# A two-stage mixture-of-experts kernel: part of the second to last expert's slots written back as whole rows by one scatter

## The chip, the cores and the metric

The kernel runs on one core of one Trainium2 chip. The metric is the device time of one execution in microseconds (us). Engines are named as the profile names them: PE is TensorE's matmul, PEld its weight load, DVE VectorE, ACT ScalarE, POOL GpSimd, SP SyncE. A small q behind a name (POOLq) is the engine's sequencer.

## What is computed

Three stages follow each other: attention in which a query sees the keys of its own hash bucket, a mixture of eight experts with one expert per token, and one with two experts per token. The change lies in the last stage, whose reference is, cut to its core:

```python
N, D, E, F = 1536, 512, 8, 1024
for e in range(E):
    for k in range(2):
        mask = top2[:, k] == e
        h = np.maximum(x[mask] @ w1[e], 0.0)
        out[mask] += top2_w[mask, k, None] * (h @ w2[e])
```

So each row of `out` (512 numbers for one token) is the sum of two experts' weighted rows.

## The kernel before

**Slots.** The tokens of an expert of the second mixture are collected in DRAM (`xs2`) in a list of `CAP2` = 416 slots per expert, of which `USE2` = 408 are computed. A slot is a row of 512 numbers, the token's number and its eight expert weights. Empty slots hold a token number out of range, which an indirect DMA drops.

**One expert of the second mixture (key 8 + e).** `x2_load` (L1315 on) and `x2_rest` (L1323) load the slots' rows and the small columns behind them. Everything is computed with the model dimension on the partitions: `mm1` (L1142 to L1144) gives four pairs of hidden blocks of 128 x 408, each product in three matmuls of split float32 parts; ACT's ReLU (L1151) and DVE's residual (L1155) split each pair and free its PSUM buffer (two buffers "S"). `mm2` (L1177 to L1179) gives four output blocks `Y` of 128 x 408; ACT copies each to SBUF (`ys`, L1202) and fills the last 8 columns (L1204). ACT and DVE also split each expert's weights (L272, L278).

**Writing back, experts 0 to 6.** `y2_turn` (L1360) turns each of the four `ys` on DVE in blocks of 32 x 32 into `yo`, so that a partition holds a quarter of a token's row for each of NQ = 13 groups of 32 slots. `y2_weight` (L1365) multiplies by the expert weight, in three parts (5, 4 and 4 groups). `y2_add` (L1368) issues one indirect DMA on POOL for each group: 128 quarter rows of 512 bytes, added to `out` by the DMA. The experts' weight columns are laid out on the host so that the quarters come out in order.

**Writing back, expert 7 (the last).** It adds on the core instead. `y2_gather` (L1342) gathers four lots of 104 rows of `out` into SBUF by indirect DMAs on POOL; they need all of expert 6's scatters to have landed. `y2_tr` (L1351) turns three lots of output on PE into PSUM; the fourth is computed by `mm2_rows` (L1189 to L1191) with tokens on the partitions, in two halves. `y2_sum` (L1356) and `y2_half` (L1196) on DVE form weight x output + gathered row, and `y2_put` (L1379) writes whole rows by four plain indirect DMAs on POOL. These puts are the last work of the kernel.

**The order.** Instructions are not issued in the order of the source. A planner (`Plan`, L104) takes steps with an engine, an expected length, a due time, dependences and buffers, and simulates the engines: each engine takes of the steps that could start within a small time (`WAITS2`, per engine) the one with the earliest due time. `LENGTH` and `LENGTH2` replace expected lengths, `SHIFT` and `SHIFT2` shift due times of groups of steps. One plan orders attention and routing (`LENGTH`, `SHIFT`, `WAITS`), a second all sixteen experts (`LENGTH2`, `SHIFT2`, `WAITS2`). What comes out is the order of each engine's queue, in which the chip then works strictly.

Of the kernel before, what the change touches and what calls it, by code (L numbers as in the profile page):

```python
# [9 lines left out]
F32 = mybir.dt.float32  # L10
F32R = mybir.dt.float32r
I32 = mybir.dt.int32
U32 = mybir.dt.uint32
AF = mybir.ActivationFunctionType
OP = mybir.AluOpType
# [6 lines left out]
N, D, E, F = NB * S, NHEAD * DH, 8, 1024  # L22
# [3 lines left out]
CAP2 = 416  # L26
USE2 = 408
MB = CAP2 // 4
ML = USE2 - 3 * MB
NQ = CAP2 // 32  # L30
RW1 = D + 2 + E
RW2 = D + 1 + E
# [5 lines left out]
HOP = {("PE", "ACT"): 260, ("PE", "DVE"): 280, ("ACT", "DVE"): 149, ("ACT", "POOL"): 195, ("DVE", "POOL"): 169,  # L38
       ("POOL", "ACT"): 86, ("ACT", "PE"): 165, ("DVE", "PE"): 228, ("DVE", "SP"): 110, ("POOL", "DVE"): 80,
       ("DVE", "ACT"): 150, ("POOL", "PE"): 100, ("ACT", "SP"): 60, ("POOL", "SP"): 60, ("PE", "POOL"): 280}  # L40
LENGTH = {('X4', 'at', 5600): 6800, ('ACT', 'ph0', 412): 407, ('DVE', 'pl0', 469): 466, ('DVE', 'pl', 469): 477, ('DVE', 'sp', 433): 806, ('ACT', 'fk0', 733): 727,
# [31 lines left out]
SHIFT2 = {'g1a': -95, 'g1b6': -110, 'g1b7': -110, 'g2a': -175, 'g2b6': -80, 'g3a': -235, 'g3b6': -25, 'g4a': 5, 'g4b6': -140,  # L73
# [3 lines left out]
    'rhd': -135, 'rla': -10, 'rlb': -25, 'rlc': 98, 'rld': 75, 'sqa': -35, 'sqb6': -15, 'wh0a': -28, 'wh0b': 7.3,  # L77
    'wh0c': 10, 'wh1a': -20.5, 'wh1b': -100, 'wh1c': -20, 'wl0a': -31.3, 'wl0b': -5, 'wl0c': -65, 'wl1a': -14, 'wl1b': 45.4,
    'wl1c': 85, 'wr0a': -40, 'wr0b': -45, 'wr1a': -90, 'wr1b': -150, 'wr1c': 250, 'xha': -20, 'xhb': -12.003557058503825, 'xhc': 97,
    'xla': -55, 'xlb': -200, 'xloa': -10, 'xloc': 85, 'xmb': -155, 'xmc': 70, 'xta': -75, 'xtb': 41, 'yc0a': -280,  # L80
    'yc0b': -100, 'yca': -27, 'ycb': 35, 'ycc': 73, 'ycd': 50, 'yra': -25, 'yrb6': -2, 'yrb7': -65, 'ywd': 94}
WAITS2 = {'PE': (0, 0), 'ACT': (325, 0), 'DVE': (120, 0.47396423297385304), 'POOL': (1495, 0)}
WAIT = 120
ROUTING = ("rsa", "rsb", "r7", "rm", "rr0", "rr", "rq", "rp", "rn", "rv", "re", "rg", "ra", "rc", "ro", "xa", "xb", "oh", "xo")
PR = dict(sc=-5.4, mx=-8.7, ex=-5.34, pv=3.37, fin=3.38, bits=-14.64, prep=-18.57, load=-37.69, h=-17.66, l=0)
# [18 lines left out]
class Plan:  # L104
# [8 lines left out]
    def add(self, name, eng, dur, fn, due, deps=(), use=(), new=(), lat=0):  # L113
        t = self.length.get((eng, name[0], dur), dur)
        dur, lat = t if isinstance(t, tuple) else (t, lat)
        due += self.shift.get(self.group(name, eng), 0)
        self.steps[name] = (eng, dur, fn, due, tuple(deps), tuple(use) + tuple(new), tuple(new), lat)
# [68 lines left out]
def lsh_attention_moe_moe2_kernel(  # L186
# [4 lines left out]
    nc = tc.nc  # L191
    xd = tc.dram_tile([N, D], F32, name="xd")
    xs1 = tc.dram_tile([E * N, RW1], F32, name="xs1")
    xs2 = tc.dram_tile([E * N, RW2], F32, name="xs2")
# [3 lines left out]
    psp = main.enter_context(tc.tile_pool(name="psp", bufs=1, space=PSUM))  # L198
# [18 lines left out]
    idf = con.tile([128, 128], F32, name="idf")  # L217
# [227 lines left out]
    ap = lambda n, b: att.enter_context(tc.tile_pool(name=n, bufs=b))  # L445
    ld, wk, hl = ap("ld", 2), ap("wk", 2), ap("hl", HLN)
    acon, rt, rows = ap("acon", 1), ap("rt", 2), ap("rows", 1)
# [411 lines left out]
    add = plan.add  # L859
    P = lambda f, *a, **k: (lambda: f(*a, **k))  # L860
    for i, t in enumerate((3150, 3700, 3900, 4500, 5600, 6200, 6300)):
        add(("at", i), f"X{i}", t, lambda: None, -100,
            new=[(r, i // 4) for r in ("qk", "vr")] if i in (0, 4) else [])
    FIRST0 = [[("fk0",), ("fv", 0), ("hc0",), ("fv1", 0), ("fa", 0, 0)], [("hc", 0), ("fv1", 1), ("fa", 0, 1)]]
    FIRST = [[], [("mx", 0, 0)], [("mx", 0, 1)], [("mx", 0, 2)]]
    for h in range(HEADS):
        z = 12 * h
        due = lambda k, o=0.0: z + PR[k] + o
        if h > 1:
            add(("load", h), "SP", 1800, P(loads, h), due("load"), [("load", h - 1)] if h > 2 else [], lat=4500,  # L870
                new=[("qk", h), ("vr", h)])
        ld_ = ([("load", h)] if h > 1 else [("at", 4)]) + ([("ph", h - 1)] if h else [])
        nq = []
        if h == 0:
            lo, hi = slice(0, 64), slice(64, 128)
            R = [("qk", 0), ("hx", 0), ("qa", 0)]
            for c in range(2):
                add(("ph0", c) if c == 0 else ("ph", 0), "ACT", 412, P(first_h, c), -40 + c, [("at", c)], use=R if c else [],
                    new=[] if c else [("hx", 0), ("qb", 0), ("qa", 0)] + nq)
# [19 lines left out]
        else:  # L899
            add(("ph", h), "ACT", 733, P(prep_h, h), due("prep"), ld_, use=[("qk", h)], new=[("hx", h)] + nq)  # L900
            add(("hc", h), "SP", 2500, P(prep_hcopy, h), due("prep", .1), [("ph", h)], lat=3500,
                use=[("hx", h)], new=[("qb", h), ("qa", h)])
            for c in range(4):
                add(("pl", h, c), "POOL", 552, P(prep_l, h, c), due("prep", .2 + .1 * c),
                    [("ph", h)] + ([("pl", h, c - 1)] if c else []),
                    use=[("qk", h), ("hx", h)] + ([("lx", h)] if c else []), new=[] if c else [("lx", h)])
            add(("lc", h), "SP", 1250, P(prep_lcopy, h), due("prep", 1), [("pl", h, 3), ("hc", h)], lat=3000,
                use=[("lx", h), ("qb", h)])
# [414 lines left out]
    def x2_rest(e):  # L1323
        x = XM[8 + e] = yp.tile([128, NQ, RW2 - D], F32, name="xm2", bufs=3)
        if e < E - 1:
            for a in range(4):
                nc.sync.dma_start(x[32 * a:32 * a + 32], xs2[e * N:e * N + CAP2].rearrange("(b j) c -> j b c", j=32)[:, :, D:])
        else:
            nc.sync.dma_start(x[:MB, :4], xs2[e * N:e * N + CAP2].rearrange("(b p) c -> p b c", p=MB)[:, :, D:])

    def x2_meta(e):
        if e < E - 1:
            IDX[e] = yp.tile([128, NQ], I32, name="idx", bufs=3)
            nc.vector.tensor_scalar(IDX[e], XM[8 + e][:, :, 0], 4.0, quarter, op0=OP.mult, op1=OP.add)
            return
        IDX[e] = yp.tile([128, NQ], I32, name="idx", bufs=3)[:, :4]
        nc.vector.tensor_copy(IDX[e][:MB], XM[8 + e][:MB, :4, 0])
        WC[e] = yp.tile([128, 4], F32, name="wc")
        nc.vector.tensor_copy(WC[e][:MB], XM[8 + e][:MB, :4, 1 + e])
# [16 lines left out]
        nc.vector.scalar_tensor_tensor(o[:MB], P[:MB], w, GA[0][:MB, b * D:b * D + D], op0=OP.mult, op1=OP.add)  # L1356

    def y2_turn(e, d):

        nc.vector.transpose(YT[e][:, :NQ * 128].rearrange("p (b c) -> p b c", c=128)[:, :, d * 32:d * 32 + 32],  # L1360
                            YS[8 + e, d].rearrange("p (b j) -> p b j", j=32))

    def y2_weight(e, bs):
        y = YT[e][:, :NQ * 128].rearrange("p (b c) -> p b c", c=128)[:, bs]
# [55 lines left out]
    add(("gm",), "POOL", 1742, ga_new, Z[15] - 5, [("xl", 15)], new=[("xr", "ga")])  # L1420
    add(("go",), "X", 7500, lambda: None, -98)
    add(("yob",), "X1", 0, P(yt_new, "b"), -98, new=[("yo", "b")])
    add(("yo7",), "X2", 0, P(yt_new, E - 1), Z[15], [("ps", E - 2, b) for b in range(NQ)], new=[("yo", E - 1)])
    add(("iw",), "POOL", 1100, iw_init, -20)
    add(("go0",), "X0", GO, lambda: None, -98)
    for n in range(4, 128):
# [13 lines left out]
    for key in range(2 * E):  # L1440
# [120 lines left out]
        else:  # L1561
            for d in range(4 if e < E - 1 else 0):
                add(("yt", key, d), "DVE", 502, P(lambda e, d: ([yt_new(e)] if d == 0 else 0, y2_turn(e, d)), e, d), z + q * (11 + 2 * d), [("yc", key, d)] + [("yt", key, 0)] * (d > 0),
                    use=[("ys", (key, d))] + [("yo", e)] * (d > 0), new=[("yo", e)] if d == 0 else [])
            for c in range(3 if e < E - 1 else 0):
                bs = slice((0, 5, 9)[c], (5, 9, 13)[c])
                add(("yw", key, c), "DVE", 60 + 134 * (bs.stop - bs.start), P(y2_weight, e, bs), t + c, [("yt", key, d) for d in range(4)] + [("xm", key)],
                    use=[("yo", e), ("xm", e)])
                for b in range(bs.start, bs.stop):
                    add(("ps", e, b), "POOL", 1850, P(y2_add, e, b), t + b, [("yw", key, c)],  # L1570
                        use=[("yo", e), ("ix", e)], lat=2000)
            for b in range(4 if e == E - 1 else 0):
                add(("ga", e, b), "POOL", 1038, P(y2_gather, e, b), z + 8 + (b + 1) % 4,
                    [("xm", key), ("gm",)] + [("ps", e - 1, c) for c in range(NQ)], use=[("ix", e), ("xr", "ga")], lat=2000)
                O = ("O" if b % 2 else "ET", ("o", e, b))
                if (e, b) == (E - 1, 3):
                    for p in range(2):
                        O = ("ET", ("last", p))
                        add(("yt", key, b, p), "PE", 2560, P(mm2_rows, p), t + p,
                            [("rl", key, c) for c in range(4)] + [("m2", key, 3, 1)] + [("yt", key, b, 0)] * p,  # L1580
                            use=[("w1", key * 8 + 4 + 2 * p + c) for c in range(2)] + [("hh", (key, c)) for c in range(4)], new=[O])
                        add(("yo", e, b) if p else ("yo0",), "DVE", 330, P(y2_half, p), t + p, [("yt", key, b, p), ("ga", e, b), ("yo7",)] + [("yo0",)] * p,
                            use=[O, ("ix", e), ("yo", e), ("xr", "ga")])
                else:
                    add(("yt", key, b), "PE", 434, P(y2_tr, e, b), t + (1.5 * b if e < E - 1 else .2), [("yc", key, d) for d in range(4)],
                        use=[("ys", (key, d)) for d in range(4)], new=[O])
                    add(("yo", e, b), "DVE", 663, P(y2_sum, e, b), t + 1.5 * b, [("yt", key, b), ("ga", e, b), ("yo7",)],
                        use=[O, ("ix", e), ("yo", e), ("xr", "ga")])
                add(("ps", e, b), "POOL", 1038, P(y2_put, e, b), t + 1.5 * b, [("yo", e, b)],
                    use=[("yo", e), ("ix", e)], lat=2000)  # L1590
# [142 lines left out]
```

## Time and profile before

| | us |
|---|---|
| median of three runs | 756.21 |
| lowest and highest | 755.67, 757.37 |
| the profiled execution | 756.93 |
| its span in the trace | 755.2 |

The span runs from the first to the last instruction that the trace shows. A row of a timeline gives start, duration, engine, line, operation with output and inputs, count, and in brackets how long the engine had been idle and what released it.

### The profile page before, as it was taken

Reading aid. Unit: us, or ns where it says so; the run is one execution under the profiler, and the core shown is the slowest. Engines: PE = TensorE matmul, PEld = TensorE weight load, DVE = VectorE, ACT = ScalarE, POOL = GpSimd, SP = SyncE. Lnnn points to the kernel's source line nnn. Section 1 sums busy time; section 2 is a strip of 40 time slices with the busy share of each in tenths; the row PEclk is TensorE's granted clock in tenths of the full one; section 3 lists DMA queues with packets and bytes.
Section 4 is the critical chain, followed back from the end, with each engine's and each line's share of the span. In section 5 each row is a group of like instructions: output and inputs, shape, how many; then the busy total and the mean of one; then the engine's idle time right before and its main releaser. Section 6 shows DMA issues by size and latency. Waiting matters only on the chain. (4 is left out here: it accounts for less than half of the span.)

```text
span 755.2 us, 14504 instructions
## 1 busy us (share of the span) xinstructions
PE 738.8 (98%) x4827; PEld 718.9 (95%) x4827; DVE 570.1 (75%) x1251; ACT 473.8 (63%) x1037; POOL 381.9 (51%) x664
## 2 busy tenths in 40 slices
PE   8999999999999999999999999999999999999995
PEld 6999999999999899999999999999999999999994
DVE  7989989999998868988978868576676656664411
ACT  7889989898878747755657745456444444444310
POOL 6543445566666550334124352046657484858474
PEclk9999999999999999999999999999999999999998
DMA  7687887888765369786687766969979595956133
GB/s 196 185 211 216 218 216 198 245 221 202 169 159 165 137 198 256 231 258 203 197 260 207 232 213 196 208 175 260 185 180 210 133 204 136 192 126 116 14 34 85
DMA packets 142117, 140.61 MB, mean 186 GB/s; under 512 B 25901, under 2 KB 122437, under 8 KB 142037
## 3 DMA queue, kind: packets, MB, share of 16 engines
q1 hardware_dynamic: 124789, 122.94, 59.5%
q0 software_dynamic: 17248, 16.69, 11.3%
q8 instruction: 40, 0.66, 0.4%
q14 instruction: 40, 0.33, 0.2%
HBM read 88.54 MB, written 34.44 MB: 163 GB/s over the span
## 5 line engine op out<-in xcount | busy, mean ns | idle before, releaser
L1368 POOL DMA_INDIRECT out_dram<-yo,idx x91 | 152.0, 1670 | 114.7 <-DVE yo L1365 89.1
L1142 PE MATMUL S<-xh,w0h 128*128 128x224 f32 (+1 forms) x512 | 161.8, 316 | 0.0
L1143 PE MATMUL S<-xl,w0h 128*128 128x224 f32 (+1 forms) x512 | 159.1, 311 | 0.0
L1144 PE MATMUL S<-xh,w0l 128*128 128x224 f32 (+1 forms) x512 | 159.0, 311 | 0.0
L1151 ACT ACTIVATE hh<-S 128x448 fp32r<-128x448 f32 (+1 forms) x64 | 44.6, 697 | 108.2 <-PE S L1144 105.6
L698 DVE TENSOR_TENSOR el<-ET,eh 128x384 fp32r<-128x384 f32 x192 | 99.2, 551 | 6.3 <-ACT eh L692 4.8
L692 ACT ACTIVATE eh<-ET 128x384 fp32r<-128x384 f32 x192 | 91.0, 496 | 16.9 <-PE ET L688 16.4
L680 ACT ACTIVATE es<-S,mxs 128x768 f32<-128x768 f32 x96 | 95.9, 999 | 8.1 <-POOL mxs L676 4.8
L670 DVE TENSOR_REDUCE mxs<-S 128x1 f32<-128x768 f32 x96 | 91.6, 954 | 12.3 <-PE S L665 9.3
L1155 DVE SCALAR_TENSOR_TENSOR hh<-S,hh 128x448 fp32r<-128x448 f32 (+1 forms) x64 | 51.9, 811 | 62.2 <-ACT hh L1151 62.1
L1143 PEld LDWEIGHTS S<-xl,w0h 128*128 128x128 f32 x512 | 97.2, 190 | 0.5 <-DVE xl L1128 0.5
L1142 PEld LDWEIGHTS S<-xh,w0h 128*128 128x128 f32 x512 | 97.4, 190 | 0.0
L1144 PEld LDWEIGHTS S<-xh,w0l 128*128 128x128 f32 x512 | 97.2, 190 | 0.0
L278 DVE TENSOR_TENSOR w1l<-wraw,w1h 128x512 fp32r<-128x512 f32 x128 | 82.7, 687 | 11.4 <-ACT w1h L272 11.2
L688 PE MATMUL ET<-idf,es 128*128 128x128 f32 x576 | 90.0, 274 | 1.0 <-DVE el L698 1.0
L1178 PE MATMUL ET<-hh,w1h 128*128 128x408 f32 (+2 forms) x264 | 89.8, 340 | 0.0
L1179 PE MATMUL ET<-hh,w1l 128*128 128x408 f32 (+2 forms) x264 | 89.7, 340 | 0.0
L1177 PE MATMUL ET<-hh,w1h 128*128 128x408 f32 (+2 forms) x264 | 89.1, 338 | 0.0
L272 ACT ACTIVATE w1h<-wraw 128x512 fp32r<-128x512 f32 x128 | 73.2, 623 | 21.9 <-PE ET L1178 9.9
L272 ACT ACTIVATE w0h<-wraw 128x512 fp32r<-128x512 f32 (+1 forms) x152 | 78.4, 560 | 3.3 <-DMA wraw<-in_w1a_dram 1.6
L278 DVE TENSOR_TENSOR w0l<-wraw,w0h 128x512 fp32r<-128x512 f32 x120 | 77.7, 686 | 3.6 <-ACT w0h L272 3.1
L688 PEld LDWEIGHTS ET<-idf,es 128*128 128x128 f32 x576 | 71.1, 142 | 8.6 <-DVE el L698 1.5
(272 smaller groups left out, 1591.4 us busy)
## 6 DMA issues: line engine op xcount, KB each, us to landing
wraw<-in_w1a_dram SPq DMA_DIRECT2D x32, 512.0 KB, 4.1
wraw<-in_w2a_dram SPq DMA_DIRECT2D x32, 512.0 KB, 6.0
wraw<-in_w1b_dram SPq DMA_DIRECT2D x32, 512.0 KB, 4.8
wraw<-in_w2b_dram SPq DMA_DIRECT2D x32, 512.0 KB, 5.9
xs<-zrow SPq DMA_DIRECT2D x26, 260.5 KB, 4.1
xr<-xs SPq DMA_DIRECT2D x28, 208.0 KB, 4.5
qk<-in_qk_dram SPq DMA_DIRECT2D x15, 384.0 KB, 4.4
xs<-zrow SPq DMA_DIRECT2D x14, 261.0 KB, 3.7
```

The source lines that it names most:

```text
L272: nc.scalar.activation(wH[n][:, c], wraw[n][:, c], AF.Copy)
L278: eng.tensor_tensor(wL[n][:, c], wraw[n][:, c], wH[n][:, c], op=OP.subtract)
L670: nc.vector.tensor_reduce(MX[(3 * g + j) % 9][:, 0:1], SC[g, j][:, :, :384], axis=AX.XY, op=OP.max, negate=True)
L680: nc.scalar.activation(ES[g, j].rearrange("p (a b) -> p a b", a=2), SC[g, j][:, :, :384], AF.Exp, bias=mx[:, 2:3], scale=mx[:, 1:2], accum ...
L688: nc.tensor.transpose(T[:, j * 128:j * 128 + 128], ES[g, j][:, kb * 128:kb * 128 + 128], idf)
L692: nc.scalar.activation(EH[g, kb], ET[g, kb], AF.Copy)
L698: nc.vector.tensor_tensor(EL[g, kb], ET[g, kb], EH[g, kb], op=OP.subtract)
L1142: nc.tensor.matmul(o, wH[n][:, fs], xh, start=kd == 0, stop=False)
L1143: nc.tensor.matmul(o, wH[n][:, fs], xl, start=False, stop=False)
L1144: nc.tensor.matmul(o, wL[n][:, fs], xh, start=False, stop=kd == 3)
L1178: nc.tensor.matmul(P, wH[n][:, ws], hl_, start=False, stop=False)
L1368: s = nc.gpsimd.indirect_dma_start(out=out.rearrange("n (a c) -> (n a) c", a=4), out_offset=bass.IndirectOffsetOnAxis(ap=IDX[e][:, b:b + 1 ...
```

## The change

For expert 6 the slots 0 to 287 (`N6` = 9 groups of 32) are written back as before, by nine scatters. The last 128 slots (288 to 415, of which 408 to 415 are empty) take another way: `y6_tr` turns the four `ys` for them on PE into a PSUM tile "O" (four 128 x 128), `y6_weight` multiplies by the weight on DVE and brings the columns into the order of `out`, and `y6_add` adds 128 whole rows of 2 KB by one scatter on POOL. `x2_rest` and `x2_meta` load their token numbers and weights once more with a slot per partition. DVE's four turns become 9 groups wide instead of 13 and the weighting has two parts instead of three. Expert 7's gathers wait for the nine scatters and the new one. Besides, two lengths of the first plan, and `SHIFT2` and `WAITS2` of the second, get other values.

```diff
+N6 = (CAP2 - 128) // 32
-LENGTH = {('X4', 'at', 5600): 6800, ...
+LENGTH = {('X4', 'at', 5600): 5750, ...
-    ('PE', 'bq', 640): 744, ...
+    ('PE', 'bq', 640): 480, ...
-SHIFT2 = {'g1a': -95, 'g1b6': -110, 'g1b7': -110, 'g2a': -175, ...
+SHIFT2 = {'g1a': -145, 'g1b7': -255, 'g2a': -235, 'g2b6': -140, ...
-WAITS2 = {'PE': (0, 0), 'ACT': (325, 0), 'DVE': (120, 0.47396423297385304), 'POOL': (1495, 0)}
+WAITS2 = {'PE': (0, 0), 'ACT': (260, 0.9), 'DVE': (215, 0), 'POOL': (120, 1)}
@@ x2_rest
+            if e == E - 2:
+                XM["r"] = mcon.tile([128, RW2 - D], F32, name="xm6")
+                nc.sync.dma_start(XM["r"], xs2[e * N + 32 * N6:e * N + CAP2, D:])
@@ x2_meta
+            if e == E - 2:
+                IDX["r"] = mcon.tile([128, 1], I32, name="idr6")
+                nc.vector.tensor_copy(IDX["r"], XM["r"][:, 0:1])
@@ y2_turn
-        nc.vector.transpose(YT[e][:, :NQ * 128]...[:, :, d * 32:d * 32 + 32],
-                            YS[8 + e, d].rearrange("p (b j) -> p b j", j=32))
+        n = N6 if e == E - 2 else NQ
+        nc.vector.transpose(YT[e][:, :n * 128]...[:, :, d * 32:d * 32 + 32],
+                            YS[8 + e, d][:, :n * 32].rearrange("p (b j) -> p b j", j=32))
+    def y6_tr():
+        P = YO[E - 2] = psp.tile([128, 512], F32, name="O", bufs=1)
+        for d in range(4):
+            nc.tensor.transpose(P[:, d * 128:d * 128 + 128], YS[14, d][:, N6 * 32:], idf)
+    def y6_weight():
+        nc.vector.tensor_scalar(YT[E - 2][:, 3 * D:].rearrange("p (a d i) -> p d a i", a=4, i=32), YO[E - 2].rearrange("p (d a i) -> p d a i", d=4, i=32),
+                                XM["r"][:, E - 1:E], None, op0=OP.mult)
+    def y6_add():
+        e = E - 2
+        s = nc.gpsimd.indirect_dma_start(
+            out=out, out_offset=bass.IndirectOffsetOnAxis(ap=IDX["r"], axis=0),
+            in_=YT[e][:, 3 * D:], in_offset=None, bounds_check=N - 1, oob_is_err=False, compute_op=OP.add)
...
@@ steps of the second plan
+            if e == E - 2:
+                add(("yq",), "PE", 436, y6_tr, z + q * 17.3, [("yc", key, d) for d in range(4)], ...)
+                add(("yv",), "DVE", 650, y6_weight, z + q * 17.4, [("yq",), ("xm", key), ("yt", key, 0)], ...)
+                add(("pq",), "POOL", 1400, y6_add, t + 3.5, [("yv",)], use=[("yo", e), ("ix", e)], lat=2000)
-            for c in range(3 if e < E - 1 else 0):
+            for c in range(2 if e == E - 2 else 3 if e < E - 1 else 0):
@@ ("ga", e, b), expert 7's gathers
-                    [("xm", key), ("gm",)] + [("ps", e - 1, c) for c in range(NQ)], ...
+                    [("xm", key), ("gm",), ("pq",)] + [("ps", e - 1, c) for c in range(N6)], ...
```

In the plan the scatters `ps` of an expert are due at t + 0, t + 1 and so on, the new one (`pq`) at t + 3.5.

## Rows read from the trace of the kernel before

**Rows 1.** The page's first part: busy us, share of the span, instructions.
```profile
PE 738.8 (98%) x4827; PEld 718.9 (95%) x4827; DVE 570.1 (75%) x1251; ACT 473.8 (63%) x1037; POOL 381.9 (51%) x664
```

**Rows 2.** TensorE by windows: stretch, length, busy (count), clock, DMA share, GB/s.
```profile
0.00:20.00 20.00, 17.11 (x76) 1.00 0.70 187
260.00:460.00 200.00, 198.09 (x1520) 1.00 0.74 222
460.00:740.00 280.00, 280.00 (x1547) 1.00 0.70 155
```

**Rows 3.** Timeline of GpSimd, end of the kernel: start, duration, what.
```profile
709.96 1.75 POOL L1368 DMA_INDIRECT out_dram<-yo,idx  x1 [9.95 <-DVE yo L1365]
...
732.39 1.55 POOL L1368 DMA_INDIRECT out_dram<-yo,idx  x1 [0.30 <-issue]
738.70 1.14 POOL L1342 DMA_INDIRECT xr<-out_dram,idx  x1 [4.75 <-issue]
...
742.91 1.07 POOL L1342 DMA_INDIRECT xr<-out_dram,idx  x1 [0.30 <-issue]
...
748.81 1.00 POOL L1379 DMA_INDIRECT out_dram<-yo,idx  x1 [1.34 <-DVE yo L1356]
750.11 0.93 POOL L1379 DMA_INDIRECT out_dram<-yo,idx  x1 [0.30 <-issue]
```

**Rows 4.** Timeline of VectorE, expert 6's write-back and the sums of expert 7.
```profile
708.21 0.61 DVE L1360 STREAM_TRANSPOSE yo<-ys 128x416 f32<-128x416 f32 x1 [1.08 <-ACT ys L1204]
708.85 2.03 DVE L1365 TENSOR_TENSOR yo<-yo,xm 128x640 f32<-128x640 f32 x3
...
742.36 0.48 DVE L1196 SCALAR_TENSOR_TENSOR yo<-ET,wc,xr 96x256 f32<-96x256 f32 x1 [15.20 <-DMA xr<-out_dram,idx]
...
747.76 0.75 DVE L1356 SCALAR_TENSOR_TENSOR yo<-ET,wc,xr 104x512 f32<-104x512 f32 x1 [1.62 <-DMA xr<-out_dram,idx]
748.42 0.47 DVE L1196 SCALAR_TENSOR_TENSOR yo<-ET,wc,xr 96x256 f32<-96x256 f32 x1
```

**Rows 5.** Timeline of TensorE, its last instructions.
```profile
741.34 0.28 PE L1191 MATMUL ET<-w1l,hh 128*96 128x256 f32 x1
741.46 0.60 PE L1351 MATMUL ET<-idf,ys 128*104 128x128 f32 x4
741.90 0.60 PE L1351 MATMUL O<-idf,ys 128*104 128x128 f32 x4
...
745.67 0.28 PE L1191 MATMUL ET<-w1l,hh 128*96 128x256 f32 x1
```

**Rows 6.** By source line, ns min/median/max: L1368 and its landing, L1327, L1379's landing.
```profile
L1368 POOL DMA_INDIRECT out_dram<-yo,idx x91: 1548/1549/2344, 499.4 to 732.4; - x91
DMA to landing us min/median/max: 2.7/4.3/8.1
...
L1327 SPq DMA_DIRECT2D xm<-xs x28: 333/474/1338, 470.1 to 606.1; - x28
...
DMA to landing us min/median/max: 2.9/3.3/4.5
```

**Rows 7.** Timeline of ScalarE: first expert stage, then expert 6's last copy.
```profile
334.88 0.54 ACT L1151 ACTIVATE hh<-S 128x448 fp32r<-128x448 f32 x1 [1.24 <-PE S L1144]
...
336.56 1.67 ACT L272 ACTIVATE w1h<-wraw 128x512 fp32r<-128x512 f32 x3
...
707.57 0.51 ACT L1202 ACTIVATE ys<-ET 128x408 f32<-128x408 f32 x1 [1.24 <-PE ET L1179]
```

**Rows 8.** All engines by windows: PE, PEld, DVE, ACT, POOL busy (count), clock, DMA.
```profile
700.00:720.00 20.00, 20.00 (x110) 20.00 (x109) 8.87 (x13) 5.72 (x12) 8.53 (x7) 1.00 0.17 15
```

**Rows 9.** Timelines of VectorE and of TensorE, first expert stage.
```profile
335.81 0.61 DVE L1155 SCALAR_TENSOR_TENSOR hh<-S,hh 128x448 fp32r<-128x448 f32 x1
...
332.23 0.27 PE L1144 MATMUL S<-xh,w0l 128*128 128x224 f32 x1
...
333.90 0.27 PE L1144 MATMUL S<-xh,w0l 128*128 128x224 f32 x1
```

More of the change, by code (lines that the diff above doesn't have):

```diff
@@ L40 @@
        ("DVE", "ACT"): 150, ("POOL", "PE"): 100, ("ACT", "SP"): 60, ("POOL", "SP"): 60, ("PE", "POOL"): 280}
-LENGTH = {('X4', 'at', 5600): 6800, ('ACT', 'ph0', 412): 407, ('DVE', 'pl0', 469): 466, ('DVE', 'pl', 469): 477, ('DVE', 'sp', 433): 806, ('ACT', 'fk0', 733): 727,
+LENGTH = {('X4', 'at', 5600): 5750, ('ACT', 'ph0', 412): 407, ('DVE', 'pl0', 469): 466, ('DVE', 'pl', 469): 477, ('DVE', 'sp', 433): 806, ('ACT', 'fk0', 733): 727,
     ('DVE', 'fv', 469): 492, ('DVE', 'lc', 469): 474, ('ACT', 'fa', 413): 412, ('ACT', 'hc0', 413): 407, ('DVE', 'fv1', 269): 560, ('ACT', 'hc', 413): 408,
[1 row of a table removed]
[1 row of a table added]
     ('ACT', 'ph', 733): 735, ('SP', 'hc', 2500): (2600, 4700), ('POOL', 'pl', 552): 558, ('SP', 'lc', 1250): (1250, 4300), ('PE', 'bp', 580): 600, ('DVE', 'bt', 640): 604,
@@ L72 @@
     ('PE', 'yt', 2560): 2839, ('DVE', 'yo0', 330): 401, ('PE', 'f1', 430): 100, ('DVE', 'f2', 200): 310}
-SHIFT2 = {'g1a': -95, 'g1b6': -110, 'g1b7': -110, 'g2a': -175, 'g2b6': -80, 'g3a': -235, 'g3b6': -25, 'g4a': 5, 'g4b6': -140,
[3 rows of a table removed]
[L77 to L81, printed above, removed]
-WAITS2 = {'PE': (0, 0), 'ACT': (325, 0), 'DVE': (120, 0.47396423297385304), 'POOL': (1495, 0)}
+SHIFT2 = {'g1a': -145, 'g1b7': -255, 'g2a': -235, 'g2b6': -140, 'g3a': -265, 'g3b6': -75, 'g4b7': -130, 'g5a': -2, 'g5aa': -180,
+    'g8a': 14, 'g8b6': -120, 'g8b7': -55, 'g9b6': -60, 'g9b7': 25, 'gib6': -135, 'gpb6': -175, 'gpb7': -35, 'm1a': -6,
+    'm1b': 15, 'm1c': 30, 'm1d': 65, 'm2a': -5, 'm2b': 18, 'm2c': 30, 'm2d': 160, 'oh': -170, 'rha': -10.4,
+    'rhb': -245, 'rhc': -80, 'rhd': -150, 'rla': -2.6, 's2a': 140, 'sqa': -30, 'sqb6': -15, 'wh0a': -3, 'wh0b': 15,
+    'wh0c': -20, 'wh0d': -100, 'wh1a': -7, 'wh1b': -45, 'wh1d': -25, 'wi1a': 65, 'wl0a': -10, 'wl0b': 20, 'wl1a': -10,
+    'wl1b': 45, 'wl1c': 70, 'wr0b': -45, 'wr1a': -102, 'wr1b': -260, 'wr1c': 265, 'xha': -5, 'xhb': -50, 'xhc': 80,
+    'xic': -75, 'xla': -110, 'xlb': -160, 'xloa': -3, 'xmb': -310, 'xmc': 62, 'xta': -55, 'xtb': 41.4, 'xtc': 55,
+    'yc0a': -225, 'yc0b': -70, 'ycb': 5, 'ycc': 65, 'yra': -20, 'yrb6': -65, 'yrb7': -140, 'yta': 2, 'ytb': -155}
+WAITS2 = {'PE': (0, 0), 'ACT': (260, 0.9), 'DVE': (215, 0), 'POOL': (120, 1)}
 WAIT = 120
@@ L1358, in y2_turn @@
     def y2_turn(e, d):
-        nc.vector.transpose(YT[e][:, :NQ * 128].rearrange("p (b c) -> p b c", c=128)[:, :, d * 32:d * 32 + 32],
-                            YS[8 + e, d].rearrange("p (b j) -> p b j", j=32))
+        n = N6 if e == E - 2 else NQ
+        nc.vector.transpose(YT[e][:, :n * 128].rearrange("p (b c) -> p b c", c=128)[:, :, d * 32:d * 32 + 32],
+                            YS[8 + e, d][:, :n * 32].rearrange("p (b j) -> p b j", j=32))
[11 more added lines that the diff above has]
+            in_=YT[e][:, 3 * D:], in_offset=None, bounds_check=N - 1, oob_is_err=False, compute_op=OP.add)
+        for x in scat3.get(e, []):
+            tc.declare_no_dep(s.ins, x.ins, reason="rows of other tokens")
+        scat3.setdefault(e, []).append(s)
     def y2_weight(e, bs):
@@ L1422, in lsh_attention_moe_moe2_kernel @@
     add(("yob",), "X1", 0, P(yt_new, "b"), -98, new=[("yo", "b")])
-    add(("yo7",), "X2", 0, P(yt_new, E - 1), Z[15], [("ps", E - 2, b) for b in range(NQ)], new=[("yo", E - 1)])
+    add(("yo7",), "X2", 0, P(yt_new, E - 1), Z[15], [("pq",)] + [("ps", E - 2, b) for b in range(N6)], new=[("yo", E - 1)])
     add(("iw",), "POOL", 1100, iw_init, -20)
@@ L1564, in lsh_attention_moe_moe2_kernel @@
                     use=[("ys", (key, d))] + [("yo", e)] * (d > 0), new=[("yo", e)] if d == 0 else [])
-            for c in range(3 if e < E - 1 else 0):
+            if e == E - 2:
+                add(("yq",), "PE", 436, y6_tr, z + q * 17.3, [("yc", key, d) for d in range(4)], use=[("ys", (key, d)) for d in range(4)], new=[("O", "o6")])
+                add(("yv",), "DVE", 650, y6_weight, z + q * 17.4, [("yq",), ("xm", key), ("yt", key, 0)], use=[("O", "o6"), ("yo", e), ("xm", e)])
+                add(("pq",), "POOL", 1400, y6_add, t + 3.5, [("yv",)], use=[("yo", e), ("ix", e)], lat=2000)
+            for c in range(2 if e == E - 2 else 3 if e < E - 1 else 0):
                 bs = slice((0, 5, 9)[c], (5, 9, 13)[c])
@@ L1573, in lsh_attention_moe_moe2_kernel @@
                 add(("ga", e, b), "POOL", 1038, P(y2_gather, e, b), z + 8 + (b + 1) % 4,
-                    [("xm", key), ("gm",)] + [("ps", e - 1, c) for c in range(NQ)], use=[("ix", e), ("xr", "ga")], lat=2000)
+                    [("xm", key), ("gm",), ("pq",)] + [("ps", e - 1, c) for c in range(N6)], use=[("ix", e), ("xr", "ga")], lat=2000)
                 O = ("O" if b % 2 else "ET", ("o", e, b))
```

5 rows, old and new, of tables (LENGTH, SHIFT2) are left out of this document.

## Prediction

> **What bounds the kernel now.** I read the page's busy table first: TensorE is busy 738.8 of 755.2 us [rows 1]. It is the bound unless the missing 16.4 us sit where the change works. So the second view is TensorE's busy time by windows [rows 2]: 2.9 us idle in the first 20 us, 1.9 us idle in 260 to 460 (first expert stage), and nothing in 460 to 740 (nearly the whole second expert stage). From 460 to 740 a microsecond taken from any other engine is worth nothing; what is left lies ahead of these windows or at the end.
>
> The third view is GpSimd's timeline of that end [rows 3]. Expert 6 (the second to last) issues 13 scatters, the first at 709.96, the thirteenth at 732.39: a mean pitch of (732.39 - 709.96) / 12 = 1.87 us. Then GpSimd sits idle until 738.70, when expert 7's first gather starts; it has to read rows of `out` that expert 6 has added to, so it waits for the thirteenth scatter to land. Four gathers follow, the last at 742.91, then four puts of finished rows, the last two at 748.81 and 750.11. The span ends 755.2 - 750.11 = 5.09 us after the last put starts. VectorE's timeline [rows 4] says what ends last before the puts: the first sum (742.36) and the sum at 747.76 both waited for a gather. TensorE's last instructions [rows 5] end at 745.67 + 0.28 = 745.95. So some 9 us run without TensorE; the end hangs on GpSimd's queue (13 scatters, landing, 4 gathers, landing), and TensorE is done 4 us before the last put is issued. The chain of waits on the page is broken off and no help here; the two timelines stand in for it.
>
> **The change, part by part.** *Scatters of expert 6.* Thirteen become nine of the old kind and one of whole rows. The group's instructions take 1.55 us (up to 2.34) [rows 6]; with the 0.3 us between them, the pitch is the 1.87 above. For the new scatter (128 rows of 2 KB, adding) there is no row; the nearest are the plain puts of 2 KB rows at 1.0 us [rows 3] and the slowest adding scatter at 2.34. I take 1.55, since it adds as those do and has as many indices; the ends give -0.5 and +0.8 on GpSimd. The four turns of VectorE ahead of them shrink from 0.61 us to 0.61 x 9 / 13 = 0.42 [rows 4], which brings the first scatter forward by the last turn's 0.19, to 709.77. The tenth then starts at 709.77 + 9 x 1.87 = 726.6. Before it was 732.39: 5.8 us earlier on GpSimd.
>
> *What the gathers gain.* From the last scatter's start to the first gather were 738.70 - 732.39 = 6.3 us; so the gathers start at 732.9 and the fourth at 737.1. The fourth's data came 747.76 - 742.91 = 4.85 us after its start [rows 3, 4]; now at 742.0 at the latest. A landing of the new scatter at the worst 8.1 us of its group instead of 4.3 [rows 6] costs nothing, since its due time puts it in the middle of the ten, not last.
>
> *TensorE.* Four turns of 128 columns are added in expert 7's time, where nothing is idle. The same operation stands in the tail: four in 0.60 us, next group 0.44 us later (741.46 to 741.90, since the pipeline overlaps them) [rows 5]. I charge 0.44 us in full; the bounds are 0.44 and the 0.60 of the row. They wait for ScalarE's copies of expert 6, the last of which was let go by TensorE at 707.57 and ends at 708.1, with a short fill behind it [rows 7]. If they stand right behind expert 6's last matmul, TensorE waits those 0.5 us, the fill and the hand-over, up to 1 us; behind the first block of expert 7's matmuls (the planner's table has 2.2 us for it) it waits for nothing. I take 0, with 1 us as the bound. Here a rule speaks against the move. The Trainium skill (VectorE: DVE Perf Modes, The three transpose paths) gives 390 ns for a full turn on TensorE and 311 on VectorE. That figure would be 1.56 us instead of 0.44 and the sum 1.1 us worse, 754.7. The trace disagrees: its turns follow each other every 0.11 us.
>
> *VectorE, SyncE, the rest.* VectorE loses 4 x 0.19 us of turns and one of three weightings (2.03 / 3 = 0.68 us [rows 4]), and gains one weighting out of PSUM (0.48 to 0.75 us by the rows of the tail's sums [rows 4]) and a small index copy. It is busy 8.9 of 20 us there [rows 8]: zero, covered by that idle time. SyncE issues one more small load for expert 6, some 0.33 to 1.34 us [rows 6], ahead of the row and weight loads behind it; TensorE, never idle in 460 to 740, shows that these have cover, so zero; without it, 0.5 us once.
>
> *The end, anew.* The gathers are in time, so TensorE is late next. The first half of the last block ends at 741.34 + 0.28 + 0.44 = 742.06; VectorE's half sum follows to 742.5 (0.48 us, overlapping the next by some 0.08). The first group of turns ends at 741.46 + 0.60 + 0.44 = 742.5; three sums of 0.75 us at a pitch of 0.66 then end at 743.25, 743.91 and 744.57. Between a sum's end and its put were 0.3 us, between two puts back to back 1.30 us [rows 3, 4]. So the puts start at 743.57, 744.87, 746.17 and 747.47. The last half sum is ready for its put at 746.39 + 0.48 + 0.32 = 747.2, so GpSimd's own pitch is what ends it, 747.47. Before it was 750.11: a gain of 2.64 us, with the TensorE charge inside. Four puts in a row could land at the 4.5 us of the worst instead of the 2.9 of the best [rows 6]: up to +1.6, not taken, since the last put before also followed its neighbour by 1.30.
>
> *Orders anew.* All experts' steps get other due times, so the queues of four engines are reordered from the first expert on, and two durations of the attention planner change too (6800 to 5750 and 744 to 480). The trace of before can't show the new order. What it can show is the room: at best the 1.9 us idle in 260 to 460 go, and about 1 us of the 2.9 at the start; at worst as much is added again. From zero to either side I take zero.
>
> **Sum.** The profiled execution took 756.93 us, 755.2 of it span and 1.73 around it. 756.93 - 2.64 = 754.3. It lies 0.72 over the median of 756.21, against which the forecast is made: 756.21 - 2.64 = **753.6 us**. What a measurement of this kernel can tell from no change is some 0.2%, 1.5 us, so 754.7 is the line.
>
> **Rivals.** (1) *The new orders eat the gain.* TensorE has no slack in the two expert stages, and the order is hand-fed by measured times; 1.1 to 4.1 us more idle time there gives 754.7 to 757.7, in the middle **756.2**. For: every expert's queues move, though only expert 6's work changes. Against: only 1.9 us are idle now, so the planner's times fit well. (2) *Slower, by ScalarE's order in the first expert stage.* There the 24 matmuls of one hidden pair take 24 x 0.111 = 2.7 us (15 of them in 333.90 - 332.23 = 1.67), and a PSUM buffer comes free only after ReLU (0.54 us) and residual (0.61 us) [rows 7, 9]; the slack is 2.7 - 1.15 - 0.3 = 1.2 us. Three weight splits in a row take 1.67 us [rows 7]. If the new order puts such a run ahead of a ReLU, TensorE stands some 0.5 us. There are 28 such pairs in experts 1 to 7; from nine of them so hit (4.5 us) the gain is gone and the line on the other side, 757.7, is passed: **758.1**. Against: a run of three stands there now without TensorE idling, because it comes behind the ReLU. (3) *A better start.* If the shorter planned times fill TensorE's idle time in the first 20 us with head 1's work, up to 1 us more is gained: **752.6**. (4) *The tail doesn't move*, because the gathers wait for something else than expert 6's scatters: then only the 0.44 us remain, **756.65**. Against: nothing else in the trace ends between 734 and 738.7.
>
> **Chances and range.** Forecast 0.56, (1) 0.20, (2) 0.09, (3) 0.12, (4) 0.03. Of the forecast's share some 0.05 lies above 754.7 (unknown costs of the new scatter, a wait of 1 us, puts landing late). Faster: 0.56 - 0.05 + 0.12 = 0.63; same: 0.05 + 0.03 and 0.17 of (1), 0.25; slower: (2) and the rest of (1), 0.12. The range reaches down to the forecast less the 1.9 us, 751.7, and up to 756.2, past the middle of (1).
>
> **What would show it.** Right: ten scatters of expert 6, the last at about 726.6; the first gather near 733; no sum of the tail waiting for a gather; the last matmul near 746.4 and the last put near 747.5. Wrong: TensorE idle by more than 2 us in 260 to 740 (rivals 1 and 2), the gathers still behind 736, or the puts spread by waits for something new.

## The result, and the profile after

| | before | after |
|---|---|---|
| median, us (runs) | 756.79 (4) | 765.23 (4) |
| lowest and highest, us | 755.67, 758.37 | 764.76, 765.35 |
| the profiled execution, us | 756.93 | 765.32 |
| its span, us | 755.2 | 763.6 |

Of before there are four runs now, the three named ahead and one more. The ratio is 1.0109, with a 95% interval from 1.0089 to 1.0129: slower by some 8.4 us, on the side to which the prediction gave 0.12, and outside its range of 751.7 to 756.2.

The page's first part after, beside [rows 1]:

```profile
PE 742.8 (97%) x4831; PEld 722.3 (95%) x4831; DVE 567.7 (74%) x1252; ACT 472.4 (62%) x1037; POOL 384.1 (50%) x661
```

TensorE has four instructions more, and stands idle 763.6 - 742.8 = 20.8 us instead of 16.4. The totals don't say where, so read the end first, as the prediction did. These are the last instructions of GpSimd after (timeline; line numbers are those of the changed kernel: L1392 the old scatter, L1380 the new one, L1348 the gathers, L1403 the puts), then of VectorE and TensorE.

```profile
719.69 1.75 POOL L1392 DMA_INDIRECT out_dram<-yo,idx  x1 [10.08 <-DVE yo L1389]
...
727.30 1.55 POOL L1380 DMA_INDIRECT out_dram<-yo,idr  x1 [0.30 <-DMA out_dram<-yo,idx]
...
736.56 1.55 POOL L1392 DMA_INDIRECT out_dram<-yo,idx  x1 [0.30 <-issue]
741.14 1.14 POOL L1348 DMA_INDIRECT xr<-out_dram,idx  x1 [3.03 <-issue]
...
753.58 1.05 POOL L1403 DMA_INDIRECT out_dram<-yo,idx  x1 [7.15 <-DVE yo L1362]
754.94 1.03 POOL L1403 DMA_INDIRECT out_dram<-yo,idx  x1 [0.30 <-DVE yo L1362]
756.27 1.00 POOL L1403 DMA_INDIRECT out_dram<-yo,idx  x1 [0.30 <-issue]
757.58 0.94 POOL L1403 DMA_INDIRECT out_dram<-yo,idx  x1 [0.30 <-POOLq L1629]
```

```profile
752.13 0.48 DVE L1196 SCALAR_TENSOR_TENSOR yo<-ET,wc,xr 96x256 f32<-96x256 f32 x1 [14.57 <-PE ET L1191]
```

```profile
719.36 0.34 PE L1144 MATMUL S<-xh,w0l 128*128 128x408 f32 x1
719.54 0.60 PE L1372 MATMUL O<-idf,ys 128*128 128x128 f32 x4
...
720.35 0.35 PE L1144 MATMUL S<-xh,w0l 128*128 128x408 f32 x1
...
755.87 0.28 PE L1191 MATMUL ET<-w1l,hh 128*96 128x256 f32 x1
```

The tail did what it was to do. Ten scatters run at a pitch of (736.56 - 719.69) / 9 = 1.87 us where thirteen did [rows 3]; the first sum waits for TensorE, where it waited for a gather [rows 4]; four puts follow each other by 1.3 us. From TensorE's end to the last put were 750.11 - 745.95 = 4.16 us [rows 3, 5]; now 757.58 - 756.15 = 1.43. But TensorE itself ends at 755.87 + 0.28 = 756.15, 10.2 us later than before.

So the loss is TensorE's. Its windows of the two expert stages after (columns as in [rows 2]) and the longest waits in 283 to 300 (engine, what it was to write, line, releaser: total us, times, longest) show one hole:

```profile
260.00:280.00 20.00, 19.97 (x163) 1.00 0.46 152
280.00:300.00 20.00, 12.79 (x83) 0.83 0.69 179
300.00:460.00 160.00, 159.21 (x1226) 1.00 0.74 224
460.00:740.00 280.00, 279.25 (x1528) 1.00 0.72 162
```

```profile
ACT hh L1151 <- PE S L1144: 10.2, 1, 10.2
...
PE ET L1228 <- DVE ys L1207: 7.2, 1, 7.2
DVE xs L1093 <- DMA xr<-xs: 7.1, 1, 7.1
```

VectorE's queue has the rest. After:

```profile
281.31 0.39 DVE L1207 TENSOR_TENSOR ys<-ET,ys 128x224 f32<-128x224 f32 x1
281.81 1.29 DVE L278 TENSOR_TENSOR w0l<-wraw,w0h 128x512 fp32r<-128x512 f32 x2
290.23 1.29 DVE L1093 STREAM_TRANSPOSE xs<-xr 128x224 f32<-128x224 f32 x4 [7.13 <-DMA xr<-xs]
291.44 0.65 DVE L1207 TENSOR_TENSOR ys<-ET,ys 128x224 f32<-128x224 f32 x2
```

and before, the last of the output adds (L1207), the same turn (L1093), and on SyncE's queue the load of the rows that it turns (L1071):

```profile
285.80 0.39 DVE L1207 TENSOR_TENSOR ys<-ET,ys 128x224 f32<-128x224 f32 x1
...
298.40 1.28 DVE L1093 STREAM_TRANSPOSE xs<-xr 128x224 f32<-128x224 f32 x4
```

```profile
279.18 3.02 SPq L1071 DMA_DIRECT2D xr<-xs  x4
```

VectorE turns expert 2's rows in L1093 and adds expert 0's output in L1207, which frees the PSUM buffers "ET". Before, the last two adds came at 283.15 and 285.80 and the turn at 298.40. Now the turn stands ahead of both, and ahead of four splits of expert 1's weights (L278). VectorE works through its queue in order: it stands 7.1 us for rows that have not landed, and the adds stand behind it, although the copies by ScalarE that they need (L1202) had ended by 284.79. TensorE waits 7.2 us for an "ET" buffer. When the rows come shows on SyncE's queue: L1071 loads them, behind four weight loads (L263).

```profile
276.54 2.63 SPq L263 DMA_DIRECT2D wraw<-in_w1a_dram  x4
279.22 0.77 SPq L1076 DMA_DIRECT2D meta<-xs  x1
280.04 3.64 SPq L1071 DMA_DIRECT2D xr<-xs  x4
```

They are issued from 280.04 on and used at 290.23, with 2 MB of weights (four times 512 KB) ahead of them; the first of the four loads landed 8.9 us after its issue. The load was no earlier in its queue before (issued at 279.18, the first landed after 7.9 us), but there the turn came 19 us behind it. By its code, the planner took the rows to have landed: its model of the transfer queue gives a transfer to whoever is due first, and the new `SHIFT2` ('xla' from -55 to -110, 'wr0a' from -40 to none) makes expert 2's rows due ahead of three of the four weight pieces, while SyncE's own order still issues them last.

The hole costs more than its 7.2 us at once: TensorE comes back at half of its clock (windows of 4 us):

```profile
284.00:288.00 4.00, 0.64 (x5) 1.00 1.19 222
288.00:292.00 4.00, 0.15 (x1) 0.71 0.40 88
292.00:296.00 4.00, 4.00 (x19) 0.50 0.36 116
296.00:300.00 4.00, 4.00 (x36) 0.94 0.51 150
```

Granted clock 0.50 (1.2 GHz) in 292 to 296, where the same stretch of before ran at 1.00 (2.4 GHz). The first ReLU of expert 1 (ScalarE, L1151), after and then before:

```profile
297.31 0.55 ACT L1151 ACTIVATE hh<-S 128x448 fp32r<-128x448 f32 x1 [10.20 <-PE S L1144]
```

```profile
287.65 0.55 ACT L1151 ACTIVATE hh<-S 128x448 fp32r<-128x448 f32 x1
```

That is 9.66 us, 7.2 of the wait and some 2 of the clock. Those of expert 0 stand at 266.40 before and 266.39 after, expert 4's first at 358.25 and 367.16 (8.9 us), the last of all at 725.27 and 735.67 (10.4 us). So nearly the whole of the 10.2 us arises here, once. The sum over the span: +10.2 at TensorE's end, 1.43 - 4.16 = -2.73 to the last put, and +0.93 behind it (6.02 us against 5.09 [rows 3]): +8.4, as timed.

### The profile page after: what moved, and what is told of

It reads as the page before. It is cut to its first block, busy times and chain, and to the rows that moved or that the text cites. A ratio compares the mean times of both kernels' runs of the same rounds, so it can differ in the third digit from the quotient of the medians.

```text
span 763.6 us, 14510 instructions
## 1 busy us (share of the span) xinstructions
PE 742.8 (97%) x4831; PEld 722.3 (95%) x4831; DVE 567.7 (74%) x1252; ACT 472.4 (62%) x1037; POOL 384.1 (50%) x661
## 3 DMA queue, kind: packets, MB, share of 16 engines
q0 software_dynamic: 16816, 16.69, 11.1%
## 5 line engine op out<-in xcount | busy, mean ns | idle before, releaser
L1392 POOL DMA_INDIRECT out_dram<-yo,idx x87 | 144.7, 1663 | 114.3 <-DVE yo L1389 89.9
L1151 ACT ACTIVATE hh<-S 128x448 fp32r<-128x448 f32 (+1 forms) x64 | 44.5, 696 | 103.8 <-PE S L1144 103.1
L278 DVE TENSOR_TENSOR w1l<-wraw,w1h 128x512 fp32r<-128x512 f32 x128 | 82.4, 683 | 23.3 <-ACT w1h L272 23.2
L1155 DVE SCALAR_TENSOR_TENSOR hh<-S,hh 128x448 fp32r<-128x448 f32 (+1 forms) x64 | 51.9, 811 | 55.2 <-ACT hh L1151 55.0
L278 DVE TENSOR_TENSOR w0l<-wraw,w0h 128x512 fp32r<-128x512 f32 x120 | 77.3, 684 | 3.1 <-ACT w0h L272 2.0
```

Of the source, the lines that this page charges most:

```text
L278: eng.tensor_tensor(wL[n][:, c], wraw[n][:, c], wH[n][:, c], op=OP.subtract)
L1392: s = nc.gpsimd.indirect_dma_start(out=out.rearrange("n (a c) -> (n a) c", a=4), out_offset=bass.IndirectOffsetOnAxis(ap=IDX[e][:, b:b + 1 ...
```

## Experiments

**The write-back alone, and the tables alone.** The first kernel is the changed one with `LENGTH`, `SHIFT2` and `WAITS2` of before, the second the kernel before with these three of the change.

```diff
 # e1_old_tables, e12_old_tables_again: the changed kernel
-SHIFT2 = {'g1a': -145, 'g1b7': -255, ...      # likewise LENGTH, WAITS2
+SHIFT2 = {'g1a': -95, 'g1b6': -110, ...
 # e2_new_tables: the kernel before
-SHIFT2 = {'g1a': -95, 'g1b6': -110, ...       # likewise LENGTH, WAITS2
+SHIFT2 = {'g1a': -145, 'g1b7': -255, ...
```

> The change with the three tables (LENGTH, SHIFT2, WAITS2) of the kernel before: ten scatters for expert 6, but orders planned as before. Theory (the loss is one stall of VectorE's queue in the first expert stage, which the new tables made; the write-back itself gains): no wait over 1 us of TensorE in 280 to 300, 754 to 755.5 us, 1.5 to 2.5 under before. Rival A (the new scatter and turns themselves cost the time): about 765. Rival B (orders planned around the new steps are bad with any table): 758 or more.

> The kernel before with the three tables of the changed kernel and nothing else: 13 scatters for expert 6. Theory: the same stall of some 7 us at 284 to 292, then matmuls at half clock, 765 to 767 us, since the end gains nothing. Rival A (the write-back costs the time): about 757.

> The write-back alone, with all three tables of before, once more for its size in the time: by the trace of its first run (span 753.8 against 755.2) 1.4 us less than before, a ratio of 0.998; by the first timing 2.4 us, a ratio of 0.996; by the prediction's sum 2.64 us, 0.9965. The tail again: no sum waits for a gather, four puts 1.3 us apart, the end about 5.9 us behind the last put.

Measured: the write-back alone 755.37 us, ratio 0.9959 [0.9943, 0.9975], and the second time 755.09 us, 0.9978 [0.9963, 0.9994]; the tables alone 766.81 us, 1.0111 [1.0087, 1.0135]. The first is faster than both kernels, the second has the whole loss. GpSimd's end in the first run of the write-back alone, then TensorE's window and the waits of the tables alone (the line numbers of the kernels differ by a few):

```profile
726.87 1.55 POOL L1393 DMA_INDIRECT out_dram<-yo,idx  x1 [0.30 <-issue]
731.37 1.14 POOL L1349 DMA_INDIRECT xr<-out_dram,idx  x1 [2.95 <-issue]
...
747.89 0.93 POOL L1404 DMA_INDIRECT out_dram<-yo,idx  x1 [0.30 <-POOLq L1630]
```

```profile
280.00:300.00 20.00, 12.99 (x91) 0.83 0.70 184
```

```profile
PE ET L1227 <- DVE ys L1206: 7.0, 1, 7.0
DVE xs L1092 <- DMA xr<-xs: 6.7, 1, 6.7
```

So write-back and tables can be told apart, and under the tables of before the write-back gains about what was predicted. Under the new tables its gain does not show: the ratio is 1.0111 without it and 1.0109 with it, each within 0.2%, and the spans are 763.3 and 763.6 us. In these two traces TensorE ends at 754.92 without it and 756.15 with it, which takes up what the tail gains; why was not looked into.

**The one order.** In the changed kernel the turn of expert 2's rows is moved back on VectorE: behind the last output add of expert 0, or behind the second split of weight piece 11 too; or SyncE issues those rows ahead of three of the four weight pieces.

```diff
 # all three: the planned order as a list, the steps of late taken out and put in at place
+seq = [n for _, _, n in sorted(plan.starts)]
 # e3_turn_back
+late, place = [("xt", 2, 0), ("xt", 2, 1)], behind ("yc", 0, 3)
 # e5_turn_back2
+late, place = [("xt", 2, 0), ("xt", 2, 1)], behind ("wl", 11, 1)
 # e6_load_first
+late, place = [("xi", 2)], ahead of ("wi", 9)
```

> The changed kernel, its planned order kept, only the two steps that turn expert 2's rows on VectorE moved behind the last output add of expert 0. Theory (this one place is the loss: 7.2 us of idle TensorE and about 2.1 us of matmuls at half clock after it): 755.5 to 756.5 us. Rival B (the new orders lose time in many places): over 759.

> As the run with expert 2's turns moved back, but moved behind the weight splits of expert 1 that also stood behind them in VectorE's queue (behind the last split of its fourth weight piece). Theory (all that was lost lies behind this one wait): no wait of TensorE over 1 us in 280 to 300, 754.5 to 756.5 us. Rival B (the new tables lose 4 us more in other places, as the 761.9 us of the first move may be read): 759 or more.

> The changed kernel with its queues as planned, except SyncE: expert 2's rows are issued ahead of the second to fourth weight piece of expert 1, which is the order of landing that the planner took for granted. Theory (the turn isn't too early, the rows are too late, because they are issued behind 2 MB of weights): rows land by 283, the wait of VectorE goes; the three weight pieces come some 3 us later and may cost 0 to 3 us: 755.5 to 759 us. Rival (the rows wait for something other than the weights ahead of them): 764 to 766.

Behind the add alone: 761.92 us, 1.0053 [1.0030, 1.0076]. That missed: VectorE stands at the same place, and now the weight splits stand behind it.

```profile
290.16 1.29 DVE L1093 STREAM_TRANSPOSE xs<-xr 128x224 f32<-128x224 f32 x4 [4.87 <-DMA xr<-xs]
291.38 2.45 DVE L278 TENSOR_TENSOR w0l<-wraw,w0h 128x512 fp32r<-128x512 f32 x4
```

```profile
292.08 0.37 PE L1144 MATMUL S<-xh,w0l 128*128 128x224 f32 x1 [3.73 <-DVE w0l L278]
```

Behind the splits as well: 756.71 us, 0.9988 [0.9977, 1.0000], 0.2 us over what was expected. With the load ahead: 757.47 us, 0.9999 [0.9982, 1.0017]. TensorE's window in the first, then in the second, where it was 12.79 in the change:

```profile
280.00:300.00 20.00, 19.47 (x156) 1.00 0.87 242
```

```profile
280.00:300.00 20.00, 19.57 (x157) 1.00 0.80 237
```

With the load ahead the first of its four loads landed 3.9 us after its issue, instead of 8.9, and the turn keeps its place in VectorE's queue:

```profile
283.63 1.29 DVE L1093 STREAM_TRANSPOSE xs<-xr 128x224 f32<-128x224 f32 x4 [0.45 <-DMA xr<-xs]
284.84 0.65 DVE L1207 TENSOR_TENSOR ys<-ET,ys 128x224 f32<-128x224 f32 x2
```

Beside the kernel before, the whole loss of 1.09% is gone in both, by moving two steps on VectorE's queue or one on SyncE's. The cause is this wait, reached from both of its sides. To the write-back alone (0.9959 and 0.9978) some 0.1 to 0.4% are still missing. A part of it is small waits of TensorE elsewhere: its busy time in 300 to 460 is 158.02 and 157.04, against 158.73.

**Which values of the tables.** The two `SHIFT2` values named above, put into the kernel before and taken back in the changed one; then whole tables of before in the changed kernel.

```diff
 # e4_xla_ahead: the kernel before
-'wr0a': -40, 'xla': -55
+'xla': -110
 # e8_xla_back: the changed kernel
-'xla': -110
+'wr0a': -40, 'xla': -55
 # e9_shifts_back: the changed kernel
-SHIFT2 of the change
+SHIFT2 of before
 # e10_waits_back: the changed kernel
-WAITS2 of the change
+WAITS2 of before
 # e11_lengths_new: the changed kernel, SHIFT2 and WAITS2 of before; LENGTH of the change stays
```

> The kernel before with two shifts changed to those of the changed kernel: 'xla' -110 instead of -55, 'wr0a' 0 instead of -40, so that the planner takes expert 2's rows to land ahead of expert 1's weight loads. Theory (these two values make the stall): 763 to 767 us, with VectorE waiting for xr in 283 to 291. Rival B (the loss is made by the tables as a whole): within 2 us of before.

> The changed kernel with two of its shifts set back, 'xla' -55 and 'wr0a' -40, and planned with them: expert 2's rows are taken to land behind expert 1's weights. Theory: the stall goes, 754 to 757 us. Rival B (the rest of the new tables is as much to blame): 759 or more.

> The change with SHIFT2 of before; LENGTH and WAITS2 stay those of the change. Theory (the shifts alone bring VectorE's turn of expert 2's rows ahead of expert 0's last two output adds): the turn goes back behind them, TensorE has no wait of over 1 us in 280 to 300, the last matmul ends within 2 us of 746.5 and the time is 754 to 758 us. Rival (the waiting times of the planner alone bring the loss): 763 to 767 us. Rival (values fitted jointly, as with two values moved back): no stall at 284 but several smaller waits, 759 to 766 us.

> The change with WAITS2 of before; LENGTH and SHIFT2 stay those of the change. Theory (the shifts carry the stall): TensorE waits 5 to 7 us for VectorE's output add near 284, the last matmul ends 8 to 11 us behind 746.5, 763 to 768 us. Rival (the waiting times carry it): no stall, 754 to 758 us.

> The change with SHIFT2 and WAITS2 of before; only the two changed LENGTH values stay. Theory (LENGTH orders the first plan alone and bears on the first stage only): the same time as with all three tables of before within 0.3%, 754 to 757 us, with TensorE's busy time in the first 20 us within 16.5 to 17.8, and no stall at 284. Rival (better start): TensorE 0.5 us or more busier in the first 20 us than with the old tables' 17.57, and the time lower by as much.

| kernel | us | ratio and interval | TensorE busy in 280:300 |
|---|---|---|---|
| two values into before | 768.17 | 1.0130 [1.0101, 1.0158] | 14.76 |
| two values back | 765.27 | 1.0106 [1.0080, 1.0131] | 18.27 |
| all shifts back | 763.19 | 1.0081 [1.0055, 1.0107] | 18.08 |
| waiting times back | 768.16 | 1.0136 [1.0112, 1.0159] | 12.66 |
| only the lengths new | 757.11 | 1.0003 [0.9988, 1.0017] | 18.27 |

The waits in 280 to 300, first with the two values in the kernel before, then with the waiting times back:

```profile
DVE xs L1093 <- DMA xr<-xs: 6.7, 1, 6.7
```

```profile
PE ET L1228 <- DVE ys L1207: 7.3, 1, 7.3
```

The two values put into the kernel before bring VectorE's wait for the rows, and the stall stays with the waiting times back. So the shifts carry the stall, and these two suffice for it. Both kernels lose a little more than was expected (768.17 and 768.16 us, where 763 to 767 and 763 to 768 were). In the first the loss is more than the stall: expert 1's first ReLU is 8.35 us later than before (296.00), the first of the second stage 11.1 us (474.95); where those 3 us go was not followed up. Taking the two values back missed: of the stall 1.6 us are left (TensorE, ahead of 286.51), and as much is lost in other places. With all shifts back the expectation missed too, and the rival named there, many smaller waits, is what came. The longest waits of TensorE in its 255 to 470:

```profile
PE ET L1229 <- DVE lg L1250: 2.8, 3, 1.5
PE O L311 <- DVE hot L417: 2.3, 2, 1.9
PE ET L1229 <- DVE ys L1208: 2.1, 3, 0.9
```

None is longer than 1.9 us, but its windows 280 to 460 and 460 to 740 miss 6.6 and 1.3 us of busy time. Shifts fitted to the waiting times that came with them would lose in this way; no run shows the fit by itself. By the medians the new lengths cost 2.0 us against the write-back alone (757.11 against 755.09, timed together), just over the 757 that was expected; the two intervals still overlap. In the traces, those of the first plan reach into the expert stage: expert 1's first ReLU stands at 288.79 instead of 287.61, and the last of all at 726.85 instead of 725.08. There SyncE issues expert 1's weights at 276.93 instead of 275.32, and TensorE waits in 280 to 300 for VectorE, 0.68 us ahead of 285.23 and 1.06 us ahead of 294.50, where it had waited 0.15 us. That the late weights make these waits fits, but was not tested. The better start is not there: TensorE's busy time in the first 20 us is 17.16, against 17.57 and 17.74 with the old lengths.

**What the clock cost.** The changed kernel with 32 matmuls of 512 columns on zeros put where TensorE stands idle; their result is not used.

```diff
 # e7_filler, ahead of ("yt", 0, 0) in TensorE's order
+P = psp.tile([128, 512], F32, name="O", bufs=1)
+for _ in range(32):
+    nc.tensor.matmul(P, wt, wt..., start=True, stop=True)
```

> The changed kernel with 32 matmuls of 512 columns on zeros (some 7 us) in TensorE's queue just ahead of the instruction that waits 7.2 us; nothing reads them. Theory (some 2 of the 9.7 us lost are matmuls at half clock after the idle time): granted clock 1.00 throughout, 762.5 to 764 us. Rival (the matmuls behind the wait are slow for another reason, or what they lose is made up later): 765 to 766.

Measured: 765.23 us, 1.0100 [1.0074, 1.0127]. No gain, a miss, though the clock stays up:

```profile
284.00:288.00 4.00, 4.00 (x21) 1.00 1.17 271
288.00:292.00 4.00, 4.00 (x19) 1.00 0.68 145
292.00:296.00 4.00, 3.71 (x32) 1.00 0.08 18
```

Expert 1's first ReLU starts at 296.08 instead of 297.31, expert 4's at 366.78 instead of 367.16, and the first of the second expert stage at 474.47 instead of 473.82. Counted from expert 0's first ReLU (267.02 instead of 266.39) that is 1.9 us gained where the clock was low, and nothing of it left at the second stage (474.47 - 267.02 = 207.45, 473.82 - 266.39 = 207.43). So by these two traces the half clock costs nothing in the end in this kernel (the interval of the times alone would leave room for 2 us); why the lead melts is not shown. That VectorE's work, piled up behind the stall, is what sets the pace then (TensorE waits 2.0 us for `hh` of L1155 in 255 to 470, after only 0.3) fits, but was not tested by itself.

## Why the prediction was wrong

**The step that failed is "Orders anew".** It took the new order of four queues as zero, with the idle time of before as its bounds to either side (1.9 us in 260 to 460 and about 1 us at the start). The upper bound was read from TensorE's idle time in [rows 2]: "at worst as much is added again". But idle time of before bounds only what can be gained; it says nothing of what a new order can lose. That bound should have come from the waits that a new order could make: here a load that lands 9 us after its issue, at the head of VectorE's queue, with the adds behind it that free PSUM. In place of zero it measured +9.66 us at expert 1 and +10.2 at TensorE's end, of which 0.44 were foreseen for the four turns. `LENGTH`, `SHIFT2` and `WAITS2` stood in the diff; they were no side matter but the larger part of the change.

**Rival 1** (new orders eat the gain) had the right part and was bounded by the same mistake: 4.1 us at most. **Rival 2** had side and stage right, and its price wrong in kind: nine stalls of half a microsecond behind ScalarE's splits, where it was one of 7.2 us behind VectorE's wait for a DMA. **Rival 3** (a better start) did not come: TensorE's busy time of the first 20 us is 17.74 after and 17.11 before (16.53 to 17.74 in all these kernels), but expert 0's first ReLU starts at 266.39 after and 266.40 before. **Rival 4** is out: the gathers moved with the scatters.

**What was right** is seen in the write-back alone (first and second run):

| us | predicted | first | second |
|---|---|---|---|
| tenth scatter starts | 726.6 | 726.87 | 725.98 |
| first gather starts | 732.9 | 731.37 | 730.63 |
| TensorE's end | 746.39 | 746.45 | 745.56 |
| last put starts | 747.47 | 747.89 | 747.00 |
| last put to the end of the span | 5.09 | 5.91 | 6.00 |
| span | 752.56 | 753.8 | 753.0 |

The gathers came 1.5 and 2.3 us earlier than predicted, which changed nothing, since no sum waits for them. The new scatter took 1.55 us, as taken, and landed in 4.7 us in the changed kernel, between the ends considered. Its four turns took 0.60 us there, one row of [rows 5] again, and TensorE lost to them what was charged: from 719.36 to 720.35 three other matmuls stand beside them in 0.99 us, where the next three take 0.56 us. From the 390 ns that the Trainium skill (VectorE: DVE Perf Modes, The three transpose paths) gives for a turn on TensorE, in bf16, the estimate was 1.56 us; these float32 rows do not bear it out. Two sizes were off. The first half sum started 0.31 us later against TensorE's end than predicted (742.43 in the first run, 4.02 us ahead of it instead of 4.33), and with it the last put came 0.36 us later (1.44 us behind it instead of 1.08). And the puts land later, the +1.6 that was named and not taken. Of the four puts after:

```profile
DMA to landing us min/median/max: 3.9/3.9/4.9
```

The median was 3.3 before [rows 6]. The last put alone landed 2.9 us after its start before, 3.9 after and 3.8 in the first run of the write-back alone. The reason given for not taking it, that the last put before also followed its neighbour by 1.30 us, overlooked that the two ahead of that pair had long left: 2.38 us stood between the put at 748.81 [rows 3] and the one ahead of it.

```profile
746.43 1.04 POOL L1379 DMA_INDIRECT out_dram<-yo,idx  x1 [0.40 <-DVE yo L1356]
```

That four puts back to back land later fits, but no run changed their spacing alone: with the tables alone they stood 1.31 to 1.57 us apart, and the last landed in 3.2 us. The three kernels with the old write-back end 5.0 to 5.4 us behind the start of the last put, all those with the new one 5.7 to 6.3. So 2.64 us shrink to 1.4 and 2.2 in the spans; the two timings give 0.41% and 0.22%, 3.1 and 1.7 us, whose intervals both hold the 2.64.

## What to carry to other kernels

When a diff reorders queues, bound its loss not by the idle time of before but by the longest wait that the new order could put at the head of a queue: look at each instruction that waits for a DMA, count the bytes ahead of that load on its queue, and see what stands behind it. A planner's model of transfers should follow the order in which they are really issued; here it did not, and placed the user of a load too early. And measure an edit and its retuned tables apart: here the edit gained 0.2 to 0.4% under the old tables, the new tables alone lost 1.1%, and under them the edit's gain did not show.

## What the runs showed of the hardware

In the 7.2 us without a matmul the granted clock fell to 0.50, where it stands from 290 to 296 with the matmuls that follow; from 296.5 on it is 1.00 again. At 0.50, matmuls of 128x224 followed each other by 0.213 us instead of 0.111. Adding a row of 2 KB took GpSimd the same 1.55 us for 128 indices as one of 512 bytes, where a plain put of 2 KB rows takes 0.93 to 1.05. The gathers could start 741.14 - 736.56 = 4.58 us behind the last scatter, where it had been 6.3 [rows 3]: the last scatter landed 3.4 us after its start, where it had been 4.6. That is 1.2 of the 1.7 us; the rest, and why it landed sooner, was not looked into.
